# An mLSTM cell and a SwiGLU block on one core: two sigmoids, one weight request and one small store change places

## The chip, the core and the metric

The kernel runs on one core of a Trainium2 chip. The metric is the time of one launch on the device in microseconds (us), the median of several runs. A profiled execution leaves a trace beside it; its span runs from the first instruction to the last.

## The reference, cut to what matters

Inputs are q, k, v and o_gate (4 batches, 8 heads, 768 steps, 40 features), i_gate and f_gate (4, 8, 768), and the weights of the second part. All are float32 in the reference's first part; the weights w_gate and w_val (320 x 1536) and w_out (1536 x 320) are float64.

```python
for t in range(S):
    m_new = np.maximum(f_gate[:, :, t] + m, i_gate[:, :, t])
    f_stab = np.exp(f_gate[:, :, t] + m - m_new)
    i_stab = np.exp(i_gate[:, :, t] - m_new)
    m = m_new
    C = f_stab[:, :, None, None] * C + i_stab[:, :, None, None] * np.einsum('bhd,bhe->bhde', vt, kt)
    n = f_stab[:, :, None] * n + i_stab[:, :, None] * kt
    h_tilde = np.einsum('bhde,bhe->bhd', C, qt)
    nq = np.einsum('bhd,bhd->bh', n, qt)[:, :, None]
    denom = np.maximum(np.abs(nq), 1.0)
    o = 1.0 / (1.0 + np.exp(-o_gate[:, :, t]))
    y[:, :, t] = o * h_tilde / denom
# x: y as (3072 tokens, 320)
g = x @ w_gate
silu = g * (1.0 / (1.0 + np.exp(-g)))
val = x @ w_val
out = silu * val @ w_out
```

## The kernel before, in words

**Tiling.** The 768 steps are cut into 6 groups of 128 steps, so one group holds 4 x 128 = 512 tokens (a tile xT of 512 columns). The recurrence is computed in a blocked form: inside a group the scores of q and k are weighted by exponentials of gate differences, and a state C is carried between half groups. The state work of group n + 1 is laid between the matrix products of group n, in slots after each hidden block. The order of everything is written by hand; each engine runs its own instructions in that order.

**Second part.** For group g, `hidden(g, m)` computes hidden block m of 12: 20 matmuls into two PSUM banks (gate and value), SiLU on ScalarE (L653), the product on VectorE (L654). Then the output product adds over the 12 blocks: `project` one batch after the other, but for group 0 `project_all(0, after)` does all four batches together in four banks, with other work hung behind each block m in the table `after` (L755). Its four results are copied out by ScalarE (`result`, L658) and stored. The "gen" banks are four, so the next `hidden` can begin only when those copies have freed them. Two z tiles take turns, so the third copy waits for the first store.

**Weights.** They are float64 in memory and are turned into float32 on the chip, block by block. They come in 9 pieces: pieces 0 and 1 hold one hidden block each, pieces 2 to 6 two blocks each (block pairs 2-3, 4-5, 6-7, 8-9, 10-11), pieces 7 to 9 are w_out. The sixth piece is piece 5, with blocks 8 and 9. `piece_load(p)` (L140) asks for the two halves of a piece: the gate half through SP's DMA queue, the value half through ScalarE's queue for p < 6 and through SP's otherwise. A request is an instruction in its engine's order, so an engine that has to wait to place it runs nothing meanwhile. `convert(j)` makes block j: `scale` (two ScalarE instructions, L190 and L192), `join` (two VectorE instructions, L199 and L200), `rounded` (one addition, L207, on GpSimd, or on VectorE where told). The raw pieces 0, 1, 4, 5 share two buffers, so piece 4 waits for the scaling of block 0 and piece 5 for that of block 1.

**Semaphores of the loads.** The built program gives each load one of eight completion semaphores, in turn. A load must wait for the one that held its semaphore before, unless its engine already knows that one to be done. In the kernel before, by its built order, these are among the holders waited for:

| load | on | waits for |
|---|---|---|
| value half of piece 3 | ScalarE | gate half of piece 0 |
| gate half of piece 4 | SP | gate half of piece 2, scaling of block 0 |
| value half of piece 5 | ScalarE | gate half of piece 3, scaling of block 1 |
| second k_sb load of group 1 | SP | the M_dram store |

**Start of the kernel.** Group 0 has its own code (`first_...`). `sig(P)` (L463) applies the sigmoid to half of the output gates o_sb. `late_sums` and `late_maxima` scan the gates of the later groups; the running maxima M_sb are stored to M_dram (L593), from where `weights_load` (L445) reads them for every later group. `late_decay` (L283) subtracts these maxima (three VectorE instructions, L284 to L286) and takes the exponential on ScalarE (L287); `late_turns` and `decay_rows` use it after hidden block 1 and 2. The order at L589 to L611 is

```python
    sig(0)
    sig(1)
    piece_load(2, h_sb[:, NH - NKC:])
    piece_load(3, wo_sb)
    nc.sync.dma_start(out=M_dram, in_=flat(M_sb))
```

and, further on, `scale(0)`, `piece_load(4)`, `join(0)`, `rounded(0, V)`, `first_state(0, A)`, `convert(1)`, `piece_load(5)`, `late_decay()`. Behind it hidden block 0 begins, with the conversion of block 2 asked for ahead of its SiLU.

**Activation tables.** Exponential, sigmoid and SiLU each need a table of ScalarE; where the next function needs another one, a table load stands in front (ACT_TABLE_LOAD in the trace). Scaling and copies need none. In the first output product ScalarE computes sigmoids behind block 0 and again, for group 2, behind block 10, and the exponentials of group 2 (`weights_exp`, L461) behind block 9.

Of the kernel before, what the change touches and what calls it, by code (L numbers as in the profile page):

```python
# [13 lines left out]
AF = mybir.ActivationFunctionType  # L14
# [10 lines left out]
def kernel(  # L25
# [18 lines left out]
    nc = tc.nc  # L44
# [28 lines left out]
    def flat(t):  # L73
        return t.rearrange("p c t -> p (c t)")
# [4 lines left out]
    def half(i):  # L79
        return slice(i * SUB, (i + 1) * SUB)  # L80
# [15 lines left out]
    qT = const.tile([128, PP, L], F32)  # L96
# [22 lines left out]
    def copy(eng, dst, src):  # L119
        if eng is nc.scalar:  # L120
            nc.scalar.copy(dst, src)
        else:
            eng.tensor_copy(dst, src)
# [16 lines left out]
    def piece_load(p, home=None):  # L140
        kind, m, n = PIECES[p]
        if kind == "gv":
            a, d = NKC, n * 128
            src = [(slice(i * HP, (i + 1) * HP), w[:, m * 128:(m + n) * 128].rearrange("(c p) f -> p c f", p=HP))
                   for i, w in enumerate((moe_w_gate, moe_w_val))]
            queues = (nc.sync, nc.scalar if p < 6 else nc.sync)
        else:
            a, d = n, DM
            src = [(slice(0, 128), moe_w_out[m * 128:(m + n) * 128].rearrange("(a p) d -> p a d", p=128))]
            queues = (nc.sync,)  # L150
        if src[0][1].dtype == F32:
            for r, w in src:
                if kind == "o":
                    nc.sync.dma_start(out=wo_sb[r, m:m + n, :], in_=w)
                else:
                    for x in range(n):
                        nc.sync.dma_start(out=wgv_sb[r, m + x], in_=w[:, :, ts(x, 128)])
            return
        if home is None:
            raw = conv.tile([128, 4 * NKC * 128], U32, name="raw")  # L160
        else:
            raw = home.rearrange("p a t -> p (a t)").bitcast(U32)
        raw = raw[:, 0:2 * a * d]
        for (r, w), queue in zip(src, queues):
            queue.dma_start(out=raw[r].rearrange("p (a d) -> p a d", a=a), in_=w.bitcast(U32))  # L165
        words = raw.rearrange("p (a d two) -> p a d two", two=2, a=a)
        raws[p] = (words[:, :, :, 0], words[:, :, :, 1])
        split(p)
# [4 lines left out]
    def split(p):  # L173
        if p in raws:
            lo, hi = raws.pop(p)
            kind, m, n = PIECES[p]
            if kind == "gv":
                for c in range(n):
                    r = slice(c * 128, (c + 1) * 128)
                    blocks[m + c] = (lo[:, :, r], hi[:, :, r], wgv_sb[:, m + c])  # L180
            else:
                for c in range(0, n, 2):
                    blocks[NFC + (m + c) // 2] = (lo[:, c:c + 2], hi[:, c:c + 2], wo_sb[:, m + c:m + c + 2, :])

    def scale(j):
        if j in blocks:
            lo, hi, dst = blocks[j]
            a, d = hi.shape[1], hi.shape[2]
            top = conv.tile([128, NKC * 128], F32, name="top", bufs=1).rearrange("p (a d) -> p a d", a=a)
            nc.scalar.mul(top, hi.bitcast(F32), 2.0 ** -112)  # L190
            low = conv.tile([128, NKC * 128], I32, name="low").rearrange("p (a d) -> p a d", a=a)
            nc.scalar.mul(low, lo, 2.0 ** -29)  # L192
            blocks[j] = (low, top.bitcast(U32), dst)

    def join(j):
        if j in blocks:
            lo, top, dst = blocks[j]
            both = dst.bitcast(U32)
            nc.vector.tensor_scalar(both, top, scalar1=3, scalar2=None, op0=ALU.logical_shift_left)  # L199
            nc.vector.scalar_tensor_tensor(both, in0=top, scalar=0x80000000, in1=both, op0=ALU.bitwise_and,  # L200
                                           op1=ALU.bitwise_or)
            blocks[j] = (lo, dst.bitcast(I32))

    def rounded(j, eng=None):
        if j in blocks:
            lo, dst = blocks.pop(j)
            (eng or nc.gpsimd).tensor_tensor(dst, dst, lo, op=ALU.add)  # L207

    def convert(j, eng=None):
        scale(j)  # L210
        join(j)
        rounded(j, eng)
# [44 lines left out]
    M_sb = early.tile([BH, NS - 2, SUB], F32)  # L257
    m_in = early.tile([BH, NS - 2, 1], F32)
    step1 = keep1
# [23 lines left out]
    def late_decay():  # L283
        nc.vector.tensor_add(m_in[:, 0:1], M0[0:BH, end].unsqueeze(1), f0[0:BH, end].unsqueeze(1))  # L284
        nc.vector.tensor_add(m_in[:, 1:], M_sb[:, 0:NL - 1, last], f_sb[:, 0:NL - 1, last])
        nc.vector.tensor_sub(step1, m_in.to_broadcast([BH, NL, SUB]), M_sb)  # L286
        nc.scalar.activation(step1, step1, AF.Exp)  # L287

    M_dram = tc.dram_tile([BH, S - L], F32, name="M_dram")

# [33 lines left out]
    q_sq = q_sb.rearrange("p (a x) d -> p a (x d)", x=2).rearrange("p a (t d) -> p a t d", d=SQ)  # L324
# [20 lines left out]
    def small(name, n=UA):  # L345
        return bank(name)[:, 0:n * D1].rearrange("p (a d) -> p a d", d=D1)
# [11 lines left out]
    def state(s):  # L358
        return C_ring[s % 3]
# [107 lines left out]
    def burn(n, tag="cell"):  # L467
        t = bank("burn", tag)
        for _ in range(n):
            nc.tensor.matmul(t, lhsT=junk[:, 0:128], rhs=junk, start=True, stop=True)  # L470
# [77 lines left out]
    def first_state(P, eng):  # L548
        ps = small("add")
        for a in range(UA):  # L550
            for two in range(2):
                h = P * UH + 2 * a + two
                nc.tensor.matmul(ps[half(two), a, :], lhsT=k_sb[:, h, :], rhs=vw_sb[:, h, :], start=True, stop=True)
        copy(eng, state(2)[:, P * UA:(P + 1) * UA], ps)
# [25 lines left out]
    first_turn(1, q_sb, qT, (A, V))  # L580
    load(o_sb, o_gate, 0, 1)
    piece_load(0)
    piece_load(1)
    late_maxima()
    first_own(1)
# [3 lines left out]
    sig(0)  # L589
    sig(1)  # L590
    piece_load(2, h_sb[:, NH - NKC:])
    piece_load(3, wo_sb)
    nc.sync.dma_start(out=M_dram, in_=flat(M_sb))  # L593
    burn(3)
    first_own(2)
    first_own(3)
# [9 lines left out]
    first_seam(1, (A, A, V))  # L606
    rounded(0, V)
    first_state(0, A)
    convert(1)
    piece_load(5)  # L610
    late_decay()  # L611


    pair = early.tile([BH, PP], F32)
# [106 lines left out]
    run = lambda f, *a: (lambda: f(*a))  # L721
# [25 lines left out]
    def early_squares(part):  # L747
# [12 lines left out]
        4: [run(convert, 16), run(seam, 1, 0, (A, V, A, V))],  # L760
        5: [run(seam, 1, 1, (A, V, A, V)), run(convert, 17), run(weights_sub, 2, 0), run(weights_mask, 0)],
        7: [run(weights_sub, 2, 1), run(weights_mask, 1), run(load_all, k_sb, k, 2)],
        8: [run(turn_squares, q_sq, qT)],
        9: [run(weights_exp, 0), run(weights_exp, 1), run(weigh_values, G, 0), run(weigh_values, G, 1)],
        10: [run(sig, 0), run(sig, 1)],
        11: [run(early_squares, 1)],
    }
    project_all(0, after)
# [78 lines left out]
```

## Time and profile before

| | us |
|---|---|
| three runs | 558.72, 560.13, 560.26 |
| median | 560.13 |
| profiled execution, its own time | 560.56 |
| its span | 558.7 |
| TensorE busy in the span | 548.1 (98%), 4992 matmuls |
| VectorE, ScalarE, GpSimd busy | 235.8, 135.7, 106.7 |
| hidden blocks' matmuls (L648) | 319.2, 1440 of 596 ns |
| output product's matmuls (L664, L671) | 130.5 and 26.9 |
| mean granted TensorE clock | 0.996 |

TensorE is busy nearly all the time, so the table is read by asking where it isn't, and where the clock that it was granted is below 1.00. The other engines' busy time counts only where TensorE waits for them. The trace's rows name the operation, the tile written and the tile read; "SPq" and "ACTq" are requests for DMAs, whose duration is that of the request and not of the transfer. The answer on DMAs gives for each request the time from issue to landing.

### The profile page before, as it was taken

The page shows a single profiled execution, that of the slowest core. Times are in us where ns is not written, and L with a number is a line of the kernel's source. Part 1 is how long each engine was busy: PE and PEld are TensorE (multiplying, and loading weights), DVE is VectorE, ACT ScalarE, POOL GpSimd, SP SyncE. Part 2 cuts the span into 40 slices and gives each one's busy share as a digit, 9 for nine tenths or more (in the row PEclk, how much of TensorE's full clock was granted, in tenths as well). Part 3 has the DMA queues.
Part 4 walks back from the last instruction along what each step waited for, and adds up shares of the span by engine and source line. Part 5 has one row for each costly group of instructions (what it writes and reads, how often), then busy time and mean ns, then how long its engine had stood idle before and what let it go on. Part 6 is the DMA issues. An engine that isn't in the chain of part 4 may idle for free.

```text
span 558.7 us, 11598 instructions
## 1 busy us (share of the span) xinstructions
PE 548.1 (98%) x4992; PEld 320.6 (57%) x4992; DVE 235.8 (42%) x394; ACT 135.7 (24%) x203; POOL 106.7 (19%) x97
## 2 busy tenths in 40 slices
PE   9989999998999999999999999999999999999997
PEld 4945446776745576455576455566455567444475
DVE  5946686972245521545531436622435621011100
ACT  4356564435110124101015110104201010111100
POOL 2314355474011132011124001106001200000000
PEclk9999999998999999999999999999999999999999
DMA  9999996798630574462375353295000131000000
GB/s 128 178 236 227 186 278 103 147 115 121 72 47 5 84 125 101 53 73 21 59 142 111 45 53 49 41 152 109 12 2 2 29 62 42 12 1 0 2 23 23
DMA packets 223994, 45.69 MB, mean 82 GB/s; under 512 B 214504, under 2 KB 219112, under 8 KB 223944
## 3 DMA queue, kind: packets, MB, share of 16 engines
q1 hardware_dynamic: 221700, 41.46, 46.0%
q10 hardware_dynamic: 2244, 3.51, 2.6%
q8 instruction: 39, 0.64, 0.5%
q14 instruction: 11, 0.09, 0.1%
HBM read 35.68 MB, written 4.01 MB: 71 GB/s over the span
## 4 chain that ended last, share of the span: by engine, by line
PE 86%; SPq 5%; DMA 3%; DVE 2%; POOL 1%; ACT 1%; issue 1%; ACTq 0%; POOLq 0%
PE gv_ps L648 55%; PE o_ps L664 23%; SPq L117 3%; DMA wo_sb<-in_moe_w_gate_dram 3%; PE sp L332 2%; PE inter L378 2%; PE intra L383 2%; PE add L354 1%; SPq L316 1%; SPq L165 1%; DVE y_sb L395 1%; POOL wo_sb L207 1%; POOL w_sb L457 0%; PE tp_kq L297 0%; DVE wo_sb L200 0%
## 5 line engine op out<-in xcount | busy, mean ns | idle before, releaser
L648 PE MATMUL gv_ps<-xT,wgv_sb 64*128 64x512 f32 x1440 | 319.2, 596 | 5.3 <-DVE wgv_sb L207 2.1
L648 PEld LDWEIGHTS gv_ps<-xT,wgv_sb 64*128 64x128 f32 x1440 | 147.1, 188 | 157.1 <-issue 146.1
L654 DVE TENSOR_TENSOR h_sb<-sg,gv_ps 128x512 f32<-128x512 f32 x72 | 49.5, 687 | 221.2 <-ACT sg L653 221.1
L664 PE MATMUL o_ps<-wo_sb,h_sb 128*128 128x320 f32 x480 | 130.5, 433 | 0.0
L664 PEld LDWEIGHTS o_ps<-wo_sb,h_sb 128*128 128x128 f32 x480 | 90.8, 190 | 41.0 <-issue 3.8
L653 ACT ACTIVATE sg<-gv_ps 128x512 f32<-128x512 f32 x72 | 43.0, 597 | 272.9 <-PE gv_ps L648 272.8
L363 POOL TENSOR_TENSOR C<-C,dec 128x328 f32<-128x328 f32 x20 | 14.5, 737 | 143.7 <-DVE C L370 143.5
L457 POOL TENSOR_SCALAR_AFFINE_SELECT w_sb<-w_sb 64x1024 f32<-64x1024 f32 x20 | 27.8, 1389 | 57.8 <-DVE w_sb L452 56.9
L658 ACT COPY z_sb<-o_ps 128x320 f32<-128x320 f32 x24 | 10.1, 423 | 93.7 <-PE o_ps L664 92.0
L404 POOL TENSOR_TENSOR o_sb<-o_sb,y_sb 128x640 f32<-128x640 f32 x10 | 14.2, 1429 | 79.1 <-DVE y_sb L395 79.1
L671 PE MATMUL o_ps<-wo_sb,h_sb 128*128 128x320 f32 x96 | 26.9, 437 | 0.0
L452 DVE TENSOR_TENSOR w_sb<-g_T,w_sb 128x1024 f32<-128x1024 f32 x10 | 13.2, 1353 | 25.4 <-DMA w_sb<-M_dram 25.4
L427 DVE STREAM_TRANSPOSE xT<-x_sq 128x640 f32<-128x640 f32 x16 | 12.5, 822 | 22.7 <-DMA x_sq<-x_sb 22.7
L671 PEld LDWEIGHTS o_ps<-wo_sb,h_sb 128*128 128x128 f32 x96 | 17.9, 190 | 7.2
L395 DVE TENSOR_TENSOR y_sb<-y_sb,intra 64x328 f32<-64x328 f32 x40 | 19.7, 492 | 0.7
L370 DVE TENSOR_TENSOR C<-C,add 40x328 f32<-40x328 f32 (+1 forms) x36 | 17.7, 493 | 1.3 <-POOL C L363 0.4
L207 POOL TENSOR_TENSOR wgv_sb<-wgv_sb,low 128x640 int32<-128x640 int32 x8 | 12.3, 1542 | 26.0 <-DVE wgv_sb L200 17.1
L378 PEld LDWEIGHTS inter<-C,qT 64*64 64x64 f32 x640 | 10.2, 134 | 7.3 <-issue 6.1
L342 POOL TENSOR_TENSOR vw_sb<-v_sb,w_sb 128x656 f32<-128x656 f32 x10 | 12.8, 1306 | 0.4
L339 DVE TENSOR_TENSOR w_sb<-sp,w_sb 128x512 f32<-128x512 f32 x20 | 12.7, 682 | 0.1
L398 DVE TENSOR_SCALAR den<-den 128x16 f32<-128x16 f32 x10 | 12.3, 1228 | 0.3
L461 ACT ACTIVATE w_sb<-w_sb 128x1024 f32<-128x1024 f32 x10 | 10.5, 1055 | 7.4 <-POOL w_sb L457 7.4
(129 smaller groups left out, 345.8 us busy)
## 6 DMA issues: line engine op xcount, KB each, us to landing
w_sb<-M_dram SPq DMA_DIRECT2D x10, 512.0 KB, 7.2
x_sq<-x_sb SPq DMA_DIRECT2D x128, 40.0 KB, 2.0
k_sb<-in_k_dram SPq DMA_DIRECT2D x12, 320.0 KB, 6.1
v_sb<-in_v_dram SPq DMA_DIRECT2D x12, 320.0 KB, 5.6
o_sb<-in_o_gate_dram SPq DMA_DIRECT2D x12, 320.0 KB, 5.5
raw<-in_moe_w_out_dram SPq DMA_DIRECT2D x3, 1280.0 KB, 7.8
out_dram<-z_sb SPq DMA_DIRECT2D x24, 160.0 KB, 1.8
q_sb<-in_q_dram SPq DMA_DIRECT2D x32, 64.0 KB, 2.2
```

What stands on the lines that cost most here:

```text
L117: nc.sync.dma_start(out=dst[:, heads(P), 0:D], in_=tokens(a, c, P))
L207: (eng or nc.gpsimd).tensor_tensor(dst, dst, lo, op=ALU.add)
L363: nc.gpsimd.tensor_tensor(state(s + 1)[:, a], state(s)[:, a], dec[:, s - 2, a].unsqueeze(2).to_broadcast([128, UA, D1]), op=ALU.mult)
L370: nc.vector.tensor_tensor(c, c, ps[r], op=ALU.add)
L378: nc.tensor.matmul(inter[two][half(i), a, :], lhsT=qT[half(two), P * UA + a, half(i)], rhs=state(2 * n + i)[half(two), P * UA + a, :], sta ...
L395: nc.vector.tensor_tensor(t, t, intra[i][half(c)], op=ALU.add)
L457: nc.gpsimd.affine_select(w, w, compare_op=ALU.is_ge, fill=NEG, base=0, pattern=[[0, UH], [1, SUB]], channel_multiplier=-1)
L648: nc.tensor.matmul(ps[i], lhsT=wgv_sb[half(i), m, PAIRS[kc][i] if g < 2 else kc, :], rhs=x[half(i), kc, :], start=(kc == 0), stop=(kc == N ...
L653: nc.scalar.activation(sg, ps[0], AF.Silu)
L654: nc.vector.tensor_tensor(hid(g, m), sg, ps[1], op=ALU.mult)
L664: nc.tensor.matmul(p, lhsT=hid(g, m)[:, ts(u, L)], rhs=wo_sb[:, m, :], start=(m == 0), stop=(m == NFC - 1))
L671: nc.tensor.matmul(ps[u], lhsT=hid(g, m)[:, ts(u, L)], rhs=wo_sb[:, m, :], start=(m == 0), stop=(m == NFC - 1))
```

## The change

Three edits, all of order or of queue; no arithmetic is added or taken away.

1. In the first output product the two sigmoids of group 2 (`sig(0)`, `sig(1)`) go from behind block 10 to behind block 8, ahead of the exponentials behind block 9. In the built program one table load disappears there.
2. The value half of piece 5 is asked for by SP instead of ScalarE.
3. `late_decay` goes ahead of the conversion of block 1. Its exponential is taken out of it and stands behind that conversion; the store of M_sb to M_dram goes from its early place to behind the requests for piece 5.

```diff
-            queues = (nc.sync, nc.scalar if p < 6 else nc.sync)
+            queues = (nc.sync, nc.scalar if p < 5 else nc.sync)
...
         nc.vector.tensor_sub(step1, m_in.to_broadcast([BH, NL, SUB]), M_sb)
-        nc.scalar.activation(step1, step1, AF.Exp)
...
     piece_load(3, wo_sb)
-    nc.sync.dma_start(out=M_dram, in_=flat(M_sb))
     burn(3)
...
     first_state(0, A)
+    late_decay()
     convert(1)
+    nc.scalar.activation(step1, step1, AF.Exp)
     piece_load(5)
-    late_decay()
+    nc.sync.dma_start(out=M_dram, in_=flat(M_sb))
...
-        8: [run(turn_squares, q_sq, qT)],
+        8: [run(turn_squares, q_sq, qT), run(sig, 0), run(sig, 1)],
         9: [run(weights_exp, 0), run(weights_exp, 1), run(weigh_values, G, 0), run(weigh_values, G, 1)],
-        10: [run(sig, 0), run(sig, 1)],
```

On VectorE the three instructions L284 to L286 now stand ahead of block 1's joining; on ScalarE one request and one table load are gone and the exponential keeps its place behind the scaling of block 1; on SP the order is gate half of piece 4, gate half of piece 5, value half of piece 5, M_dram store, k_sb. TensorE and GpSimd keep their orders. Since the store left its early place, the loads behind it get other semaphores: the value half of piece 3 has no earlier holder to wait for, the gate half of piece 4 waits for the gate half of piece 1, the value half of piece 5 (on SP) for the gate half of piece 3, and the second k_sb load for the value half of piece 2.

## The prediction

> **What bounds the kernel now.** I read the page first (TensorE busy 98% of 558.7 us, so only what idles or slows it can move the end), then who TensorE waited for, then the chain of waits, then the stretches around each wait with the granted clock. Halves of a weight piece p are called gp (gate) and vp (value).
>
> TensorE's waits over 0.4 us, beside the warm-up's (columns: us in total, times, longest):
>
> ```profile
> PE gv_ps L648 <- DVE wgv_sb L207: 2.1, 1, 2.1
> PE gv_ps L648 <- ACT z_sb L658: 2.0, 1, 2.0
> PE gv_ps L648 <- POOL wgv_sb L207: 1.2, 1, 1.2
> ```
>
> They lie at 31.69 (block 0's weights), 43.91 (block 2's weights) and 128.88 (end of the first output product). From 50 us to 128.88 and from 130.85 to the end TensorE has no gap, so whatever is saved at the three goes to the end if no later cover breaks. The chain of waits shows what stands before the second and the third (start, us, what):
>
> ```profile
> 23.50 15.09 DMA wo_sb<-in_moe_w_gate_dram
> ...
> 38.67 0.60 ACTq L165
> ...
> 40.60 0.74 ACT keep L287
> 41.33 0.68 ACT top L190
> ...
> 43.54 1.55 POOL wgv_sb L207
> ...
> 45.13 4.80 PE gv_ps L648 x20
> ...
> 126.76 1.06 ACT w_sb L461
> ...
> 127.83 1.28 ACT L464
> ...
> 129.13 1.36 ACT o_sb L464 x2
> 130.49 0.32 ACT z_sb L658
> ...
> 130.85 19.36 PE gv_ps L648 x80
> ...
> 218.97 17.37 PE gv_ps L648 x80
> ```
>
> The reader is to see: ScalarE stood until 38.67 in front of v5's request, which waits for g3 to land; only then came the exponential, then block 2's scaling. And at 127.82, with the exponentials done, ScalarE did a table load and two sigmoids before the copy that frees TensorE's banks. The last two rows are the same 80 matmuls, 1.99 us longer after the gap than a group later. The stretches say why (PE busy, ..., granted clock in the third column from the end):
>
> ```profile
> 31.69:33.80 2.11, 0.00 (x2) 0.03 (x1) 1.93 (x4) 1.44 (x4) 0.00 (x0) 1.00 1.05 221
> 128.88:130.85 1.97, 0.00 (x1) 0.00 (x0) 1.01 (x1) 1.96 (x5) 1.39 (x2) 1.00 1.54 135
> 130.85:134.25 3.40, 3.40 (x8) 2.81 (x10) 0.00 (x0) 1.71 (x4) 2.29 (x3) 0.53 0.41 122
> ```
>
> After the third gap the clock is 0.53 for 3.40 us. That gap costs 1.97 + 1.99 = 3.96 us, not 2.
>
> **Part 1: sigmoids ahead of exponentials (first output product).** Before, the table goes SiLU, sigmoid (98.71), exponential (119.70), sigmoid (127.83). After, the two sigmoids stand behind the scaling of block 17, which ends at 117.80, and the sigmoid table is still loaded: one load of 1.28 us goes. They need o_sb, whose two loads landed at 116.6 and 118.5 (issued 110.53 and 112, 6.1 and 6.4 us). So sigmoids 118.5 to 119.9, exponential table to 121.2; the first exponential waits for GpSimd until 124.35 anyway: nothing is delayed, with 3 us in hand. The second ends at 127.82 as before. The last matmuls of the four output banks end about 0.27 us apart (26.04 / 96), the first bank at 128.1: copy 128.2 to 128.6, the next to 128.95. TensorE ends at 128.88 and goes on at once: 1.97 us saved. With no gap I take the clock drop away too: 1.99.
> Here the Trainium skill speaks against me: TensorE: Matmul & The Clock Gate, Part 1: The HAM clock gate (the "warmup" mystery), has the clock halved only after an idle window of about 3.4 us. By that, 1.97 us of idling need not be the cause, and the sum would be 1.97. The row shows half clock directly behind the gap and nowhere else; yet the 2.11 us gap at 31.69 has clock 1.00 behind it. I take the row, 3.96, and keep 1.97 as a case.
> What is late next: copies 3 and 4 wait for the stores of copies 1 and 2 (1.64 us before). These would now queue behind the second k_sb load, which was moving to 131; copy 4 then ends near 133.6, when the second pair of banks is due (129.0 + 4.36 = 133.35). Price 0 to 0.5, I take 0.2. Part 1: 3.7.
>
> **Part 2: v5 asked for by SP.** It removes ScalarE's stand from 35.36 (scaling of block 1) to 38.67 and the 0.60 us of issue. But block 2's scaling needs g2 and v2: v2 was issued at 25.71 and took 13.7 us, landing at 39.4. So its start goes from 41.24 to 39.4, not to 37. TensorE followed the start by 45.13 - 41.24 = 3.89 us; after: 43.3, 1.8 us sooner. Its own readiness bounds this: first block plus second took 33.80 to 43.91; it cannot gain more than the gap of 1.2 plus what block 0 gains.
> Block 0 gains by a side effect. The built program hands eight completion semaphores to the loads in turn, and a load waits for the earlier holder. With the M_dram store gone from its place all later loads move one holder on: v3, which waited for g0 (landed at 28.69, issued at 28.79 with ScalarE behind it), waits for nothing. ScalarE copies at about 27.0 instead of 29.43, scales block 0 when g0 lands (28.75 instead of 30.39), and TensorE starts at about 32.2 instead of 33.80: 1.6. It is then ready at 42.3; block 2 at 43.3 leaves a gap of 1.0. So the two are not added: 1.8 in all. If v3 did not move, still 1.2.
> On SP: g4 waits for g1 (30.5) rather than g2 (33.65); g5 follows at about 34; v5 waits for g3 (38.6), and behind it stand the M_dram store, k, q, g6, v6 and the w_sb loads. The first k_sb load goes from 36.03 to about 39.9, but the queue then still holds g4 and g5, so it does not run dry. v5 in one queue behind g5, instead of beside it, may cost 3.3 us of that queue (640 KB at 197 GB/s). Covers: q landed at 59.2 and is turned at 64.2 and 69.6; v6 at 65.5 for a scaling at 71.70; v5 itself at 50.9 for one at 62.88; the M_dram store, even at 15 us, lands at 54.3 ahead of its reader at 57.1. All hold with 3.3 later there and 1.8 sooner here. The tightest is w_sb: about 68.7, to 72.0, for VectorE at 71.60 - 1.8 = 69.8; the product h behind it (76.49 to 77.17) would be 0.4 later than before while TensorE wants the bank at 77.6. Price 0 to 0.5, taken at 0.
>
> **Part 3: subtraction ahead of block 1's joining; exponential and store split off.** The three VectorE instructions (0.14, 0.15, 2.18 us; the last beside a GpSimd addition) now stand after block 0's addition at 32.1. At the old prices joining 1 ends at 36.0 and GpSimd's addition at 37.7, where TensorE wants block 1 at about 37.8: nothing, just covered; GpSimd is idle at 32.1, so I expect the 2.18 nearer 0.8. The exponential (1.28 + 0.74) runs on ScalarE at 34 to 36, inside the wait for v2. The store's absence ahead of v2 can only help v2.
>
> **Sum.** 3.7 + 1.8 = 5.5. The profiled execution took 560.56 us at a span of 558.7; 560.56 - 5.5 = 555.1. Its time is 0.43 above the median of the three runs (560.13), so 554.6.
>
> **Rivals.** *A, v2 lands later:* if it lands near 41.2, part 2 gives nothing: 556.4. For it: g4 is asked for 3 us sooner and shares the engines. Against: v2 and v3 are still asked first. If v2 lands by 38.3 the gap vanishes and part 2 gives 2.9: 553.5.
> *B, the clock drop does not follow from the gap, or the usual run has none:* 1.97 instead of 3.96: 556.6. For it: the page's window, the gap at 31.69, and one of the three runs at 558.72.
> *D, slower: ScalarE's queue is starved.* From 27 to 31 us only SP's queue moved weights, while v2 had been asked for at 25.71:
>
> ```profile
> DMA packets 481, 0.79 MB, mean 197 GB/s; under 512 B 25, under 2 KB 175, under 8 KB 480
> ...
> q1 hardware_dynamic: 480, 0.78, 108.3%
> ```
>
> If v2 must wait until SP's queue has no more weights, g4, g5 and v5 now come first: 3 x 3.3 us, v2 lands at 49.3, TensorE starts block 2 at 53.2, 8.1 late, plus some 2 for the clock, less 3.7: 566.5. It decides from a landing at 46.6 on (two of the three ahead of it). Against it: from 36 to 39 us ScalarE's queue moved 0.58 MB and SP's 0.04, though g4 had been asked for at 33.76: each queue got its turn in order of asking. The Trainium skill says likewise (DMA: Bandwidth & Descriptors, Queues, rings and completion order: an engine goes round the queues, a packet at a time); by that rule v2 would even have shared from 26 us, which the row denies, so I don't rule D out.
> *C, nothing moves:* A and B together with a late w_sb: 558.5 to 561.8.
>
> **Chances.** Main case 50% (553.6 to 555.6), early v2 8%, A 15%, B 14%, C 6%, D 7%. A measurement here can tell about 0.3% (1.7 us) from no change. Faster: 50 + 8 + 15 + 14 = 87%; same 6%; slower 7%. The range 552.5 to 558.3 holds all but C and D.
>
> **What would show it.** Right: no TensorE wait for z_sb, clock 1.00 behind the first output product, group 1's first 80 matmuls near 17.4 us; no ScalarE wait for wo_sb's load; block 2 begun near 43.3; later stages 5 to 6 us sooner. Wrong: v2 landing after 41; a wait for w_sb or q_sb between 60 and 85 us that reaches TensorE; sigmoids held past 122 by o_sb.

## The result, and the profile after

The changed kernel took 555.17 us in the median of four runs (553.87 to 555.24); the kernel before, beside it, took 559.57 us (the three runs shown ahead and a fourth of 559.0). The ratio is 0.9917 with a 95% interval of 0.9894 to 0.9939, so the gain is 3.4 to 5.9 us, where 5.5 had been reckoned. The profiled execution took 555.16 us at a span of 553.0 us, against 560.56 and 558.7 before.

Who TensorE waited for in the changed kernel (us in total, times, longest; the warm-up's row and two rows of 0.2 us are left out):

```profile
PE gv_ps L648 <- POOL wgv_sb L207: 1.1, 1, 1.1
PE gv_ps L648 <- DVE m_in L285: 0.5, 1, 0.5
PE intra L382 <- issue: 0.3, 1, 0.3
```

Of the three waits before, that for z_sb is gone, that ahead of block 0 fell from 2.1 to 0.5, and that ahead of block 2 is nearly as long as it was, 1.1. A new one stands in the matmuls `intra` of the second half group. The row for block 0 names `m_in` (L285) because that small VectorE instruction now stands right behind the addition of block 0; block 0 began 0.14 us after that addition's end (0.15 before), so it was not held up by it.

The chain of waits of the changed kernel (start, us, what):

```profile
25.43 13.59 DMA h_sb<-in_moe_w_val_dram
...
39.17 0.81 ACT top L190
...
41.51 1.54 POOL wgv_sb L207
43.10 4.80 PE gv_ps L648 x20
...
100.08 0.56 PE intra L382 x34
100.65 0.33 issue
100.98 0.67 PE intra L382 x27
...
114.34 13.12 PE o_ps L671 x48
127.46 17.38 PE gv_ps L648 x80
```

v2 lands at 39.0, and only this holds block 2 now: ScalarE begins its scaling at 39.17 and TensorE its matmuls at 43.10. At the other end, the last output matmuls pass at once into group 1, and its first 80 matmuls take 17.38 us. The stretches from there on show that the clock stayed whole (granted clock in the third column from the end):

```profile
127.39:130.80 3.41, 3.41 (x17) 1.66 (x18) 0.76 (x1) 0.00 (x0) 3.16 (x4) 1.00 1.21 168
130.80:135.00 4.20, 4.20 (x22) 2.09 (x20) 0.69 (x1) 2.69 (x4) 0.61 (x1) 1.00 0.55 125
```

Followed along TensorE's starts, from before to after: block 0 33.80 to 31.90; block 2 45.13 to 43.10, so 2.03 sooner; the second `intra` 101.92 to 99.89, still 2.03 sooner; the output matmul behind it 103.00 to 101.58, only 1.42 sooner; group 1 130.85 to 127.39, 3.46 sooner; the last copy 555.35 to 549.99, 5.36 sooner. The remaining 0.3 of the span's 5.7 lies behind that copy (3.35 us to the end before, 3.01 after).

### The profile page after: what moved, and what is told of

Same layout as the page of the kernel before. It is cut to its first block, busy times and chain, and to the rows that moved or that the text cites. A ratio compares the mean times of both kernels' runs of the same rounds, so it can differ in the third digit from the quotient of the medians.

```text
span 553.0 us, 11595 instructions
## 1 busy us (share of the span) xinstructions
PE 546.4 (99%) x4992; PEld 312.9 (57%) x4992; DVE 234.4 (42%) x394; ACT 134.7 (24%) x202; POOL 106.6 (19%) x97
## 4 chain that ended last, share of the span: by engine, by line
PE 92%; DMA 4%; SPq 3%; POOL 0%; DVE 0%; ACT 0%; issue 0%; ACTq 0%; POOLq 0%
PE gv_ps L648 55%; PE o_ps L664 24%; PE o_ps L671 5%; SPq L117 3%; DMA h_sb<-in_moe_w_val_dram 2%; PE inter L377 2%; PE sp L331 2%; PE intra L382 2%; DMA o_sb<-in_o_gate_dram 2%; PE add L353 1%; PE tp_kq L296 0%; POOL wgv_sb L207 0%; PE tp_x L439 0%; DVE wgv_sb L200 0%; ACT top L190 0%
## 5 line engine op out<-in xcount | busy, mean ns | idle before, releaser
L648 PEld LDWEIGHTS gv_ps<-xT,wgv_sb 64*128 64x128 f32 x1440 | 139.1, 187 | 159.4 <-issue 154.6
```

The source lines that it names most:

```text
L648: nc.tensor.matmul(ps[i], lhsT=wgv_sb[half(i), m, PAIRS[kc][i] if g < 2 else kc, :], rhs=x[half(i), kc, :], start=(kc == 0), stop=(kc == N ...
```

## The experiments

Each ratio is to the kernel before on the same chip, with a 95% interval. The first four, the next four and the last four each shared their runs of before.

**The sigmoids alone.**

```diff
-        8: [run(turn_squares, q_sq, qT)],
+        8: [run(turn_squares, q_sq, qT), run(sig, 0), run(sig, 1)],
...
-        10: [run(sig, 0), run(sig, 1)],
```

> The kernel before with the sigmoids' move alone. My theory (the idle gap behind the first output product costs its 1.97 us and the clock drop behind it 1.99 us more): no TensorE wait for z_sb, clock 1.00 behind it, group 1's first 80 hidden matmuls near 17.4 us, 3.9 us faster than before, near 555.7. Rival B (the clock drop has another cause): only the idle 1.97 us goes, the 80 matmuls stay near 19.4 us, near 557.6.

Measured: 557.18 us, ratio 0.9954 [0.9931, 0.9977], some 2.6 us. There is no wait for z_sb, and block 2 still waits. From its waits and its chain:

```profile
PE gv_ps L648 <- POOL wgv_sb L207: 1.7, 1, 1.7
...
128.19 17.48 PE gv_ps L648 x80
```

Edit 1 is worth about half of the whole. The gain lies between the two expectations (3.9 and 2.0 us) and its interval, 1.3 to 3.9 us, does not part them.

**The gap filled instead of removed.** The kernel before, with eight matmuls added that nothing uses, where TensorE would wait for z_sb.

```diff
-        11: [run(early_squares, 1)],
+        11: [run(early_squares, 1), run(burn, 8)],
```

> The kernel before with 8 dummy bf16 matmuls (of the kind that warm TensorE up at the start, about 0.2 us each, nothing reads them) behind block 11 of the first output product, that is, inside the gap before group 1; the wait for the copies stays. My theory (the clock falls because TensorE idles there): clock 1.00 behind the gap, group 1's first 80 matmuls near 17.4 us instead of 19.4, 2.0 us faster than before though TensorE's real work restarts no sooner, near 557.6. Rival B: the clock falls all the same, no change, near 559.6.

Measured: 559.08 us, ratio 0.9997 [0.9974, 1.002]: no difference in time that can be told, where 2.0 us had been expected. In its profile the 80 matmuls behind the filled gap took 17.76 us at clock 1.00, though group 1 began no sooner than a z_sb copy let it (the half clock of this execution lies at 25 to 31 us):

```profile
130.12 17.76 PE gv_ps L648 x80
```

So of the 1.99 us by which the 80 matmuls were longer than 17.37 before, 0.39 is there without any lowered clock.

**v5 on SP alone.**

```diff
-            queues = (nc.sync, nc.scalar if p < 6 else nc.sync)
+            queues = (nc.sync, nc.scalar if p < 5 else nc.sync)
```

> The kernel before with v5's request moved to SP alone. My theory: ScalarE scales block 2 when v2 lands at 39.4 instead of at 41.2; block 0 keeps its start of 33.8, since v3 still waits for g0, so TensorE is ready for block 2 at 43.9 and finds it done (43.3): the gap of 1.2 us goes, 1.2 us faster, near 558.4. Rival (what part 2 gained comes from the store and the order, not from this queue): under 0.4 us.

Measured: 560.55 us, ratio 1.0018 [0.9995, 1.0042]. No gain; the expected 1.2 us are outside the interval. Its profile (565.41 us) has two stretches at half clock (34.5 to 37.9 and 137 to 140 us), so only its waits are read. TensorE's:

```profile
PE gv_ps L648 <- ACT z_sb L658: 2.0, 1, 2.0
PE intra L383 <- issue: 1.5, 1, 1.5
...
PE gv_ps L648 <- DVE h_sb L654: 1.1, 1, 1.1
```

and VectorE's between 60 and 85 us:

```profile
DVE w_sb L452 <- DMA w_sb<-M_dram: 4.0, 1, 4.0
```

Block 2 no longer waits, but the bound has moved down SP's queue: w_sb comes 4.0 us late for VectorE, the product h_sb behind it keeps TensorE for 1.1, and the stop in `intra` is 1.5. Nor did the request alone clear ScalarE's way. With the subtraction in its late place, the exponential had to wait for it, and the scaling of block 2 stood behind both:

```profile
39.50 0.74 ACT L287 ACTIVATE keep<-keep 32x640 f32<-32x640 f32 x1 [1.80 <-DVE keep L286]
40.15 0.76 ACT L190 ACTIVATE top<-h_sb 128x640 f32<-128x640 f32 x1
```

**Edit 3 alone, v5 left on ScalarE.**

```diff
-        nc.scalar.activation(step1, step1, AF.Exp)
...
-    nc.sync.dma_start(out=M_dram, in_=flat(M_sb))
...
+    late_decay()
     convert(1)
+    nc.scalar.activation(step1, step1, AF.Exp)
     piece_load(5)
-    late_decay()
+    nc.sync.dma_start(out=M_dram, in_=flat(M_sb))
```

> The kernel before with the third edit alone: subtraction ahead of block 1's joining, exponential ahead of v5's request, M_dram store behind it; v5 stays in ScalarE's queue. Theory 1 (v2's landing bounds block 2): the exponential runs at 34 to 36, v5's request goes out when g3 lands at about 38 and is done before v2 lands at about 39, so ScalarE loses nothing by it: block 2 begins near 43.2, block 0 near 32, 2.0 us faster, near 557.6, as much as edits 2 and 3 together. Theory 2 (v5 has to leave ScalarE's queue): ScalarE still stands, block 2's scaling does not begin before 40.5, under 0.8 us faster.

Measured: 557.65 us, ratio 0.9955 [0.9934, 0.9977], some 2.5 us. ScalarE in its timeline:

```profile
25.36 0.63 ACTq L165 DMA_DIRECT2D wo_sb<-in_moe_w_val_dram  x1
...
34.99 0.74 ACT L609 ACTIVATE keep<-keep 32x640 f32<-32x640 f32 x1
38.24 0.60 ACTq L165 DMA_DIRECT2D raw<-in_moe_w_val_dram  x1
38.96 0.78 ACT L190 ACTIVATE top<-h_sb 128x640 f32<-128x640 f32 x1 [3.24 <-DMA wo_sb<-in_moe_w_gate_dram]
```

v3 is asked for at 25.36 instead of 28.79, and v5 still stands in front of block 2's scaling until 38.24. But the exponential is already done, so the scaling begins at 38.96 (41.24 before) and block 2 at 42.86. This is as soon as in the changed kernel, with v5's request still on ScalarE.

**The changed kernel once more.** No edit against it.

> The changed kernel once more, on the chip of the next three, to compare them with. Both theories: 0.8% below before; TensorE's waits 1.1 us for block 2 and about 0.5 for block 0, VectorE's wait of 1.3 us for w_sb again, TensorE's stop inside the second intra product (0.3 us) again if it comes from the later SP queue, gone if it was chance.

Measured: 554.68 us, ratio 0.9895 [0.9862, 0.9928]. Block 2 began at 42.41, after a wait of 0.3 (1.1 expected); the stop in `intra` came again and is here 0.59.

**The changed kernel with v5 back on ScalarE**, that is edits 1 and 3 without edit 2.

```diff
-            queues = (nc.sync, nc.scalar if p < 5 else nc.sync)
+            queues = (nc.sync, nc.scalar if p < 6 else nc.sync)
```

> The changed kernel with v5's request back in ScalarE's queue, that is, edits 1 and 3 without edit 2. Theory 1 (edit 2 gains nothing once the exponential stands ahead of the request, and delays SP's queue): no VectorE wait for w_sb, no stop in the second intra product, block 2 begun no later than in the changed kernel; 0 to 0.8 us faster than the changed kernel. Theory 2 (v5 has to leave ScalarE's queue): block 2 later by 0.6 or more, slower than the changed kernel.

Measured: 554.67 us, ratio 0.9896 [0.9862, 0.993]: equal to the changed kernel beside it. Its only wait of TensorE over 0.2 us behind the start-up is

```profile
PE gv_ps L648 <- DVE m_in L285: 0.3, 1, 0.3
```

There is no gap at block 2 (v2 was asked for 1.1 us sooner in this execution, when o_sb had landed, and landed near 37.5), no stop in `intra`, and VectorE waits 0.2 for w_sb. With the run of v5 on SP alone this says that edit 2 brings nothing that can be told, by itself or with the others.

**v2 and v3 asked for ahead of the second start-up sigmoid**, on top of that version, to move the bound that is left.

```diff
     sig(0)
-    sig(1)
     piece_load(2, h_sb[:, NH - NKC:])
     piece_load(3, wo_sb)
+    sig(1)
```

> f2 with the requests for v2 and v3 on ScalarE ahead of the second sigmoid at the start, so that v2 is asked for at about 22.4 instead of 25.4. My theory (block 2 waits for v2's landing at 39): v2 lands near 36, block 2 is ready before TensorE, its wait of about 1 us goes: 0.7 to 1.1 us faster than f2. Rival (the engines serve what was asked first on SP's queue, so v2 still lands near 39, or delays g0 and g1 instead): 0 or slower, and block 0 begins later.

Measured: 558.57 us, ratio 0.9944 [0.9911, 0.9976]; its runs lie in two groups, 554.2 to 554.9 and 558.5 to 560.7, beside one of 562.6 that the ratio leaves out. The expected gain over the version without this edit did not come. v2 was asked for at 21.21 and landed 3.6 us sooner, at 33.9, yet block 2's scaling began at 39.28, because v5's request stood ahead of it until g3 had landed (38.55). Moving the load did not move the stage; TensorE had no wait there either, since block 0 began only at 33.65 (31.73 in the version without this edit), its transposes of x having run at half clock. Its profiled execution was at half clock from 26.5 to 30.2, and by its mean clock each of its runs had at least one such stretch. It is not a better kernel.

**The changed kernel with the store back in its early place.**

```diff
     piece_load(3, wo_sb)
+    nc.sync.dma_start(out=M_dram, in_=flat(M_sb))
...
     piece_load(5)
-    nc.sync.dma_start(out=M_dram, in_=flat(M_sb))
```

> The changed kernel with the M_dram store put back to its early place, all else as changed. My theory (the store's leaving shifts the loads' semaphores, so that v3 no longer waits for g0): v3's request waits for g0 again, ScalarE's first copies come behind it, block 0 begins 1.0 to 1.6 us later than in the changed kernel; as block 2 then waits for nothing, 0.5 to 0.8 us slower than the changed kernel. Rival (the store itself, in SP's queue ahead of v2, was the delay): v2 lands later by more than 0.5 us, block 2 with it.

Measured: 557.9 us, ratio 0.9958 [0.9933, 0.9983], 3.2 us above the changed kernel beside it (554.68), where 0.5 to 0.8 had been expected. Its profiled execution took 560.78 us, 2.9 above the median, with half clock from 32 to 39 us and o_sb landing 1.8 us later than in the changed kernel, so its starts are not compared. Its waits show that v3 waits for g0 again (asked for at 30.79, 3.58 behind v2; 0.64 in the changed kernel) and that the transposes of x wait for ScalarE behind it:

```profile
PE tp_x L561 <- ACT xT L121: 2.0, 1, 2.0
...
PE gv_ps L648 <- DVE m_in L285: 1.2, 1, 1.2
PE gv_ps L648 <- DVE h_sb L654: 1.0, 1, 1.0
```

The third row is w_sb once more, 3.9 us late for VectorE here: on SP, g4 was asked for at 35.8 (30.3 in the changed kernel) and everything behind it later. The clock is not what makes the 3.2 us: the five runs with a mean clock of 0.999 or more took 556.55 to 557.87, the four such runs of the changed kernel 553.63 to 554.73. The rival finds no support, as v2 took 13.9 us from its request to its landing, 13.6 in the changed kernel. One line for 80 KB is worth more here than edit 2.

**The store moved alone**, in the kernel before.

```diff
     piece_load(3, wo_sb)
-    nc.sync.dma_start(out=M_dram, in_=flat(M_sb))
...
     piece_load(5)
+    nc.sync.dma_start(out=M_dram, in_=flat(M_sb))
     late_decay()
```

> The kernel before with one line moved: the store of M_sb to M_dram stands behind the requests for piece 5; order on ScalarE and VectorE and both queues as before. Theory 1 (the store's place gives the loads other semaphores, v3 no longer waits for g0): v3 asked for near 26 instead of 28.8 us, block 0 begins near 32.0 instead of 33.8, TensorE ready for block 2 near 42.1; v5's request still stands ahead of the exponential and of block 2's scaling, so block 2 begins near 43.5 with a gap of 1 to 1.5; time 1.2 to 1.7 us below before. Theory 2 (it is the order of exponential and request that brings edit 3's 2.5 us): block 0 may move, block 2 stays at 45.1, time within 0.5 us of before.

Measured: 558.52 us, ratio 0.9987 [0.997, 1.0004]: no gain that can be told. Block 0 moved as theory 1 says, but both theories missed the rest. From the chain of waits of this kernel:

```profile
32.00 4.56 PE gv_ps L648 x20
...
37.62 9.27 PE gv_ps L648 x40
...
67.69 13.95 PE gv_ps L648 x60
...
100.67 0.62 issue
```

The 40 matmuls from 37.62 are block 1 and block 2 without a gap: block 2 begins 3 us sooner than before. By the built order the semaphores shifted so that v5 waits here for g2, not for g3; it was asked for at 33.61, and ScalarE's stand of 3 us went too. Most of the gain was then given back: the 60 matmuls from 67.69 take 13.95 us (12.93 before), because w_sb comes late, and `intra` stops for 0.62. VectorE's wait in the stretch from 55 to 85 us:

```profile
DVE w_sb L452 <- DMA w_sb<-M_dram: 2.8, 1, 2.8
```

Group 1 began at 129.76, only 1.1 sooner than before. The lateness can be followed: here it is g5's request on SP that waits for g3 (6.8 us, until 37.3; with edit 3 complete and v5 on ScalarE g5 was asked for at 33.7), so w_sb was asked for at 56.94, against 55.16 there. In the changed kernel, with v5 in g5's place, it was 56.61 and w_sb 1.3 us late; TensorE is 1.0 us further ahead here, which makes about 2.6 of the 2.8 us.

**The order alone**: the subtraction ahead of block 1's joining and the exponential ahead of v5's request, the store in its early place.

```diff
+    late_decay()
     convert(1)
+    nc.scalar.activation(step1, step1, AF.Exp)
     piece_load(5)
-    late_decay()
```

> The kernel before with the rest of edit 3: the subtraction ahead of block 1's joining, the exponential ahead of piece 5's request; the store in its early place, v5 on ScalarE. Theory 1: v3 still waits for g0 (asked for near 28.8), block 0 begins at 33.5 to 33.8; the scaling of block 2 follows v5's request at once, near 39.3 instead of 41.3, so block 2 has no gap and begins near 43.8: time 1.2 us below before. Theory 2: block 2 near 43, time 2 to 2.5 us below before. If the two halves of edit 3 add up to edit 3's 2.5 us, each has about half; if either alone gives 0, they only work together.

Measured: 558.51 us, ratio 0.9975 [0.9954, 0.9995], some 1.4 us. The semaphores moved here too: v5 waits for no load and was asked for at 33.77; block 2's scaling began at 38.61, block 2 at 42.52, and nothing was lost later: group 1 began at 128.26. v3 does wait for g0, but g0 had landed early in this execution, so it was asked for at 27.17 and block 0 began at 32.18. As v5 has another holder in either half, the two runs do not part the exponential's place from v5's wait.

**Edit 3 with eight unneeded matmuls in the gap, and edit 3 again.** The first adds the eight matmuls, as further above, to edit 3; the second is edit 3 unchanged.

> Edit 3 alone (order and store) with eight unneeded matmuls of 512 columns added behind block 11 of the first output product, where TensorE waits 2 us for z_sb. Theory 1 (the idle 2 us are what lowers the clock in some executions): no execution has half clock directly behind it; mean of the runs 0.5 to 1.2 us below edit 3 alone, runs with two stretches of half clock gone. Theory 2 (half clock comes from elsewhere, at random): the shares of runs with none, one and two stretches are as with edit 3 alone, time within 0.4 us of it.

> Edit 3 alone once more, for the three beside it: ratio to before 0.994 to 0.997 as at its first run. Theory 1: it equals the sum of what its two halves give alone (about 2.5 us); theory 2: it equals one of them.

Measured: with the dummies 556.83 us (555.94 to 557.84), ratio 0.9952 [0.9933, 0.9972]; without 558.08 us (556.09 to 559.16), ratio 0.997 [0.9954, 0.9986]. The medians are 1.2 us apart although the dummies shorten nothing, but the intervals overlap, and edit 3's first run had 0.9955 without dummies: a saving in time is not shown. Nor is it settled whether edit 3's halves add up: they gave 0.7 and 1.4 us, edit 3 gave 1.7 here and 2.5 at first. Edit 3's first run and this one give one kernel and one gap, once without and once with a lowered clock behind it. The stretch behind the gap in the first,

```profile
128.70:132.10 3.40, 3.40 (x15) 2.42 (x17) 0.00 (x0) 1.71 (x4) 1.96 (x3) 1.00 0.34 117
```

and in the second:

```profile
128.70:132.10 3.40, 3.37 (x8) 2.81 (x10) 0.00 (x0) 1.71 (x4) 2.06 (x3) 0.52 0.35 115
```

The 80 matmuls took 17.76 us in the first and 19.31 in the second, so the lowered clock costs 1.55 us where it comes. Behind the dummies the 80 matmuls took 17.76 as well; that execution's half clock lies at 25 to 31 us.

## Why the prediction came out as it did

**The gap at z_sb: right.** 1.97 us went, and so did the lengthening behind it: 3.94 us were gained from the end of the output product on (1.42 to 5.36), where the sum had 3.7. The sigmoids ran at 116.25, the exponentials ended at 126.40, and the copies followed without a table load. The 0.2 us priced for copies 3 and 4 did not come in this execution: they waited 3.80 us for the stores, and the 80 matmuls still took 17.38. With v5 back on ScalarE they waited 4.3 us, and the 80 matmuls took 17.91 at clock 1.00, 0.54 more than 17.37, so such a price can come.

**The 1.99 us behind it: right in sum, wrong in name.** The text put all of it down to the clock. 0.39 us of it comes with the gap whatever the clock (17.76 against 17.37); it fits the third and fourth z copies coming late, which is argued and not tested. 1.55 us is the clock, and it comes in some executions of a kernel and not in others. The profile of before happened to have it, so that the sum of the two profiles came out at 3.94 is in part luck: edit 1 alone gave 2.6 us in the runs' times. Rival B (the usual run has no drop) was half true. By the mean clocks, none of the 7 runs of edit 3 with the gap filled had two stretches of half clock, and 10 of the 24 runs of edit 3 without dummies did; of the kernel before it was 2 of 12 with the gap filled and 13 of 32 beside them without. Where the gap is gone, in the changed kernel and in the version with v5 back on ScalarE, none of 16 runs had two. That makes the gap a likely cause of one stretch, by chance from run to run.

**v2 as the bound of block 2: right.** Expected 39.4 for the landing, 43.3 for block 2 and 32.2 for block 0; the trace has 39.0, 43.10 and 31.90. Rivals A and D did not occur.

**The step that named the cause: wrong.** Part 2 was headed "v5 asked for by SP" and gave it the 1.8 us, with the store's place as a side effect and 1.2 us if v3 did not move. That case was measured (v5 on SP alone, the store in its early place) and gave nothing; edits 1 and 3 without edit 2 took the time of the whole change. What brings part 2's gain is edit 3, priced at nothing as part 3: the exponential is out of the way before v2 lands, so ScalarE may stand in front of v5's request as long as it likes up to about 39 us, and the store's late place keeps v3 from waiting for g0. The sum held by luck: both edits lead to the same bound, v2's landing, and the working took that bound from one and left the other out. What inside edit 3 counts for how much stays open, since each half alone gave v5 another semaphore and so brought block 2 to about 42 us.

**w_sb as the tightest cover: right, with a limit now.** Expected 2.2 us late for VectorE and 0 to 0.5 us of TensorE; the changed kernel has 1.3 us late (1.7 in its second profile) and no loss. The store moved alone had it 2.8 late and lost 1.02, the changed kernel with the store early 3.9 and lost 1.0, v5 on SP alone 4.0 and lost 1.1. So 1.7 us of lateness is free and 2.8 is not, and edit 2 brings the kernel near that edge: with v5 back on ScalarE w_sb was 0.2 late.

**Not foreseen: the stop in `intra`.** Of the 2.03 us won at block 2 TensorE lost 0.61 in the second half group, 0.33 of it shown as a stop behind 34 of 64 matmuls and the rest in a slower run on either side. It was priced nowhere, and between the two profiles the total (5.7 us of span) came out close to 5.5 by chance, because part 1 was a little larger than its price and 0.3 us came off behind the last copy.

**Part 3:** the subtraction L286 took 0.81 us (2.18 before, 0.8 expected), and it held nothing up. That its price was nothing is the error above: it is the part that pays.

## What to carry to other kernels

Before a request is moved to another queue, look for what stands behind it in its old one: here it was enough to take the short exponential out from behind the wait, and the request could stay. In a program that hands its semaphores out in turn, as this one does, a moved DMA also changes which older load each later load has to wait for, so its cost is read from the waits of the loads behind it and not from its bytes. And ask of each saved microsecond what is next: with 2 to 3 us taken off the front of this kernel, a transfer at the end of SP's queue and a stop in the middle of a matmul group took 0.6 to 1.9 us back.

## What the runs showed of the hardware

**Half clock in stretches of 3.4 us.** They lie behind gaps (before block 0, behind the z_sb wait) or in the transposes ahead of block 0, and come or stay away between executions of one kernel; two can follow each other, as with the store back in its early place (32 to 39 us). Half of 3.41 us over 558 us is 0.003 of the mean clock, so a run's mean clock counts them: the 85 runs of before had none in 8, one in 51 and two or more in 26, and in the first of the three sets their median times were 558.8, 560.0 and 562.4. In the other two sets one stretch made no difference (559.1 and 558.9; 558.9 and 559.1) and two or more cost 2 to 4 us, so the clock is not all that differs between runs. The Trainium skill (TensorE: Matmul & The Clock Gate, Part 1: The HAM clock gate (the "warmup" mystery)) gives a free-running window of 3413 ns, which the 3.40 us rows fit, and a lowered clock only behind an idle window of about 3.4 us. The second does not hold here: the drop of 0.52 stands behind a gap of 1.99 us, and the same gap had none in another execution.

**A stop that follows a large transfer.** The second `intra` stops behind its 34th matmul when it comes soon behind the request for w_out's third and last piece of 1280 KB. Distance from that request to its start, and the stop:

| kernel | us from request to `intra` | stop, us |
|---|---|---|
| v5 on SP alone | 5.81 | 1.52 |
| changed kernel, second profile | 6.36 | 0.59 |
| store moved alone | 6.39 | 0.62 |
| changed kernel | 6.80 | 0.33 |
| store early, else as changed | 6.90 | none (64 matmuls in 1.31) |
| order alone | 7.00 | none (1.15) |
| v5 back on ScalarE | 7.62 | none (1.12) |
| before | 7.84 | none (1.15) |
| the other six profiles | 7.07 to 8.95 | none |

A packet of the instruction queue moves at the end of that transfer; in the changed kernel, from 98 to 99 us:

```profile
q1 hardware_dynamic: 60, 0.11, 29.3%
q8 instruction: 1, 0.02, 6.8%
```

and `intra` goes on 2.4 to 2.7 us behind it in all four stopped executions. In the ten profiles without a stop the packet had moved 2.5 to 3.9 us before the 34 matmuls were done, in the four with one 1.0 to 2.4 us before. So TensorE seems to wait for its own next instructions behind the weights. The order of the table and these distances speak for it; no run took the transfer away, so it is not shown.

**One queue alone is slow.** Each queue fills half of the partitions. With SP's queue alone 197 GB/s moved (27 to 31 us, shown with the prediction); from 41 to 46 us before, with both, 0.89 and 0.86 MB in 5 us, or 350 GB/s. From 36 to 39 us before, with nearly all of it through ScalarE's queue, it was 207. That the half of the partitions is the reason was not tested.
